# Gated values in PSUM banks, a bank seeded by a bank copy, and a new order of products and down products

## The chip, the cores and the metric

The kernel runs on one core of a Trainium2 chip. The metric is the device time of one execution in microseconds. Before the change it was 1130.64 us, the median of three runs (1128.69 to 1130.8).

## What is computed

A masked attention is followed by two gated feed-forward layers over 2304 tokens of 512 features, with 1536 hidden units in 12 chunks of 128. The second layer has no norm. Cut to what matters here:

```python
def _moe2_ref(x, w_gate, w_val, w_out):
    g = x @ w_gate
    silu = g * (1.0 / (1.0 + np.exp(-g)))
    val = x @ w_val
    return silu * val @ w_out
```

All is float32. The kernel makes each factor of a product the sum of a high and a low part (`xh` and `xl`, `hh` and `hl`, two planes of a weight tile) and multiplies three of the four pairs.

## The kernel before

The first part of the program runs the attention together with chunks 0 to 5 of the first layer. The change doesn't touch it. The second part goes through a list `work` of 15 blocks. A block is 768 tokens with a group of chunks: two passes of three chunks for the rest of the first layer (`m` is 1), then three passes of four chunks for the second (`m` is 2), each pass over three blocks of tokens. Block n uses one set of four PSUM banks for its chunks (`gv`) and the other (`ya`) for the down products of its first half; they change places at the next block.

A `Chunk` computes gate and value for the two halves of 384 tokens with seven products instead of eight, by sums of blocks of x and of the weights. `step(i)` issues product i, six matmuls, and what hangs on it. A chunk has two banks, x and y. Products 1, 6, 7 and 4 go to x one upon the other, and ScalarE copies x out in between (`keep`, L985): t1 after 1, t2 after 6, t3 after 7. Product 2 starts y anew; VectorE adds y to t1 (`add`, L990), and ScalarE makes silu of it (L994), which is the gate of the first half. Product 5 starts y anew again; y is added to t3, the value of the second half. Product 3 goes on top of 5; y is added to t2, the value of the first half. After product 4 ScalarE makes silu of x into t4, the gate of the second half. `join` multiplies gate and value on VectorE (L998), ScalarE rounds the result to `hh` (L1002), and VectorE makes the difference `hl` (L1003).

`Half.down` multiplies `hh` and `hl` of a half with a slice j of the down weights and sums over the chunks in bank y[j]; the last chunk's call adds what the pass before left (`evict`, L1080), in a tile `ob` that `fetch` (L1053) has filled from DRAM, and stores it (L1097). The x of the next block is loaded by `stage_x` (L939, one buffer), summed on POOL (L946, L947) and split product by product (`split_q`): ScalarE writes `xh` (L961), POOL makes sums (L955, L957) and `xl` (L962). Between these the weights of the next pass are decoded in steps that `point()` starts: DMA, ScalarE (L184, L185), VectorE (L190, L191), POOL (L235), ScalarE (L195), VectorE (L199).

The order of the code sets most of the order on each engine; a scheduler moves instructions within it by priorities (`ahead`, `behind`). Every engine, and the DMA queue of SP, serves its instructions in order. For one chunk and the next the order before is: product 1 of the next, 7 of this, 2 of the next, 6 of the next, 4 of this, 5 of the next, 3 of this, with down products between. At the last chunk 7, 4 and 3 follow with the down products of an earlier chunk between 7 and 4.

Of the kernel before, what the change touches and what calls it, by code (L numbers as in the profile page):

```python
# [25 lines left out]
def attn_ffn_ffn(ctx: ExitStack, tc: tile.TileContext, q, k, v, w1g, w1v, w1o, rms_g, w2g, w2v, w2o, out):  # L26
    nc = tc.nc
# [901 lines left out]
    x7, xs, tp, obp = (pools[key][0] for key in ("x7", "xs", "t", "ob"))  # L929
# [38 lines left out]
    class Chunk:  # L968
# [19 lines left out]
        @ahead  # L988
        def add(self, t):
            last["dve"] = ins_of(nc.vector.tensor_tensor(out=t, in0=t, in1=self.y[:, :HN], op=ALU.add))  # L990
# [5 lines left out]
        @ahead  # L996
        def join(self, s, v, half):
            nc.vector.tensor_tensor(out=s, in0=s, in1=v, op=ALU.mult)  # L998
            n = (3, 4)[half]
            hh = tp.tile([128, HN], F32R, tag=f"hh{half}", name="hh", bufs=n)  # L1000
            hl = tp.tile([128, HN], F32R, tag=f"hl{half}", name="hl", bufs=n)
            last["act"] = ins_of(nc.scalar.copy(out=hh, in_=s))  # L1002
            last["dve"] = ins_of(nc.vector.tensor_tensor(out=hl, in0=s, in1=hh.bitcast(F32), op=ALU.subtract))  # L1003
            return hh, hl

        def step(self, i):
            if i == 1:
# [3 lines left out]
                self.ga = self.keep("t1", 3)  # L1011
            elif i == 2:
                self.y = bank(self.tags[1])
                self.mult(self.y, 2, True)
                self.add(self.ga)
                self.silu(self.ga, self.ga)
            elif i == 6:
                self.mult(self.x, 6, False)
                self.va = self.keep("t2", 2)
            elif i == 5:  # L1020
                self.y = bank(self.tags[1])
                self.mult(self.y, 5, True)
            elif i == 7:
                self.mult(self.x, 7, False)
                self.vb = self.keep("t3", 2)
                self.add(self.vb)
            elif i == 4:
                self.mult(self.x, 4, False)
                gb = tmp("t4", 1)
                self.silu(gb, self.x[:, :HN])  # L1030
                self.hb = self.join(gb, self.vb, 1)
            elif i == 3:
                self.mult(self.y, 3, False)
                self.add(self.va)
                self.ha = self.join(self.ga, self.va, 0)
            point()

    class Half:

        def __init__(self, m, t0, tags, cs, before, after):  # L1040
# [4 lines left out]

        @ahead
        def fetch(self, j):
            if self.before is None:
                return
            ob = self.ob[j] = obp.tile([128, 512], F32, tag="ob", name="ob")  # L1050
# [24 lines left out]
        def evict(self, j):  # L1075
# [5 lines left out]
            else:  # L1081
                ob = obp.tile([128, 512], F32, tag="ob", name="ob")
# [21 lines left out]
    for n, (m, cs, t0) in enumerate(work):  # L1104
# [7 lines left out]
        halves = [Half(m, t0, ya, cs, before, after), Half(m, t0 + HN, gv[other:] + gv[:other], cs, before, after)]  # L1112
# [3 lines left out]
        def lower(c, js):  # L1116
            for j in js:
                halves[0].down(c.c, j, c.ha)
            point()
# [5 lines left out]
        def head_step(c, z):  # L1125
# [4 lines left out]
        def tail_step(c, z):  # L1130
            c.step(z)
            if c is chunks[-1]:
                split_next(z)

        def lower_at(i, js):
            if i >= 0:
                lower(chunks[i], js)

        def spread(js):
            for j in js:  # L1140
                for c in chunks[:-1]:
                    halves[1].down(c.c, j, c.hb)
                point()

        for z in (1, 2, 6):
            chunks[0].step(z)
            if left:
                left.pop(0)()
        for i, c in enumerate(chunks[:-1]):
            c1 = chunks[i + 1]  # L1150
            head_step(c1, 1)
            if i == 0:
                c.step(5)
                if nxt:
                    cell = stage_x(nxt[0], nxt[2])
                    sum_x(cell)
            tail_step(c, 7)
            head_step(c1, 2)
            lower_at(i - 2, J[:2])
            head_step(c1, 6)  # L1160
            tail_step(c, 4)
            head_step(c1, 5)
            tail_step(c, 3)
            lower_at(i - 2, J[2:])
            if t0 + 2 * HN == NT:
                used((m, c.c, False))
        for j in J:
            halves[0].fetch(j)
        tail_step(chunks[-1], 7)
        lower_at(k - 3, J)  # L1170
        tail_step(chunks[-1], 4)
        tail_step(chunks[-1], 3)
        if t0 + 2 * HN == NT:
            used((m, cs[-1], False))
        spread(J[:2])
        lower_at(k - 2, J)
        spread(J[2:])
        if t0 + 2 * HN == NT:
            for c in cs[:-1]:
                used((m, c, True))  # L1180
        lower_at(k - 1, J)
        for j in J:
            halves[1].fetch(j)

        def tailpiece(hf, c, js, done):
# [8 lines left out]
        def finished(m=m, c=cs[-1], t0=t0):  # L1194
            if t0 + 2 * HN == NT:
                used((m, c, True))

        js = [list(J[:2])] + [[j] for j in J[2:]]
        left = [tailpiece(halves[1], chunks[-1], g, finished if g is js[-1] else None) for g in js]
        left.pop(0)()  # L1200
        if nxt is None:
            while left:
                left.pop(0)()
# [31 lines left out]
```

## Time and profile before

| | |
|---|---|
| median of three runs | 1130.64 us |
| the profiled execution's own time | 1125.63 us |
| its span | 1123.9 us |
| TensorE matmul, weight load | 1018.3 us (91%), 919.3 us (82%) |
| VectorE | 721.1 us (64%) |
| ScalarE | 583.3 us (52%) |
| POOL | 484.1 us (43%) |
| DMA | 133.85 MB, 119 GB/s on the mean |

PE is TensorE's matmul, PEld its weight load, DVE VectorE, ACT ScalarE, POOL GpSimd, SP the queue that issues the DMAs. L66 is the line that issues every matmul. Matmuls overlap, so the duration of one is longer than the time from one start to the next, and a busy TensorE is not one at its peak. An instruction's row says how long its engine was idle ahead of it and what ended that.

### The profile page before, as it was taken

To read this page: it belongs to the slowest core of one execution; us is meant where nothing else is said; L and a number is where in the kernel's file an instruction comes from. 1 tells how busy PE (TensorE), PEld (TensorE's weight loads), DVE (VectorE), ACT (ScalarE), POOL (GpSimd) and SP (SyncE) were. 2 spreads that over 40 slices of the span, in tenths; PEclk is the share of its full clock that TensorE was granted. 3 is DMA by queue.
4 is the path that set the end of the run, shared out by engine and by line. 5 is a ranking of instruction groups with operands and counts; after the bars stand their busy time and mean duration, and the time that the engine had idled before them with its cause. 6 is when DMAs were issued, how large, how long until landed. Compare 5 with 4: busy or idle time off the path is not lost.

```text
span 1123.9 us, 16427 instructions
## 1 busy us (share of the span) xinstructions
PE 1018.3 (91%) x5804; PEld 919.3 (82%) x5804; DVE 721.1 (64%) x1361; ACT 583.3 (52%) x1435; POOL 484.1 (43%) x407
## 2 busy tenths in 40 slices
PE   5769999999999997998799799999889998979997
PEld 4569998777898787988699688879777987979896
DVE  3687464454436787669965887446978458894543
ACT  5877656366235573454634655436563427462431
POOL 3213112021001345667756848273856355583700
PEclk8758999999999998998899999999899999899999
DMA  7683152231233453353463271321253341615032
GB/s 198 174 225 104 61 159 65 80 98 38 61 118 114 149 160 96 111 184 123 163 199 121 74 234 39 131 93 58 85 178 114 130 146 61 207 55 169 2 113 75
DMA packets 130090, 133.85 MB, mean 119 GB/s; under 512 B 41428, under 2 KB 113820, under 8 KB 130008
## 3 DMA queue, kind: packets, MB, share of 16 engines
q1 hardware_dynamic: 129816, 132.53, 37.5%
q8 instruction: 45, 0.74, 0.3%
q0 software_dynamic: 192, 0.28, 0.1%
q14 instruction: 37, 0.30, 0.1%
HBM read 99.75 MB, written 33.03 MB: 118 GB/s over the span
## 4 chain that ended last, share of the span: by engine, by line
PE 45%; DVE 20%; DMA 16%; ACT 7%; POOL 6%; issue 3%; SPq 2%; DVEq 0%; ACTq 0%; POOLq 0%
PE b_y L66 16%; PE b_a L66 10%; PE b_g L66 9%; PE b_v L66 9%; DMA raw<-in_moe_w_out_dram 4%; POOL xl L962 4%; DMA part<-ob 4%; DVE t L998 3%; DVE hl L1003 3%; DVE dh L191 3%; DVE raw L190 3%; DVE w L199 3%; DMA ob<-part 2%; DVE t L990 2%; PE b_a L69 2%
## 5 line engine op out<-in xcount | busy, mean ns | idle before, releaser
L962 POOL TENSOR_TENSOR xl<-xst,xh 128x384 fp32r<-128x384 f32 x168 | 211.8, 1285 | 118.7 <-PE b_y L66 54.5
L66 PE MATMUL b_y<-xh,w 128*128 128x384 f32 x700 | 193.0, 346 | 31.2 <-DVE t L990 21.0
L66 PEld LDWEIGHTS b_y<-xh,w 128*128 128x128 f32 x700 | 130.7, 193 | 39.2 <-DVE t L990 25.3
L66 PE MATMUL b_g<-xh,w 128*128 128x384 f32 (+2 forms) x496 | 150.4, 351 | 7.1 <-ACT t L985 6.0
L66 PE MATMUL b_v<-xh,w 128*128 128x384 f32 (+2 forms) x432 | 132.5, 356 | 13.8 <-DVE t L990 13.8
L66 PE MATMUL b_a<-xh,w 128*128 128x384 f32 (+2 forms) x460 | 131.9, 341 | 13.6 <-DVE t L990 7.6
L998 DVE TENSOR_TENSOR t<-t,t 128x384 f32<-128x384 f32 x108 | 102.9, 955 | 49.2 <-ACT t L994 47.9
L1003 DVE TENSOR_TENSOR hl<-t,hh 128x384 fp32r<-128x384 f32 x108 | 107.3, 1004 | 25.8 <-ACT hh L1002 25.2
L66 PE MATMUL b_y<-hh,w 128*128 128x256 f32 (+2 forms) x432 | 120.1, 349 | 1.8 <-ACT hh L744 1.8
L66 PE MATMUL b_y<-xl,w 128*128 128x384 f32 x350 | 119.5, 341 | 0.0
L66 PEld LDWEIGHTS b_g<-xh,w 128*128 128x128 f32 x496 | 91.9, 193 | 16.7 <-ACT t L985 8.0
L66 PEld LDWEIGHTS b_a<-xh,w 128*128 128x128 f32 x460 | 84.5, 190 | 19.8 <-DVE t L990 9.5
L66 PEld LDWEIGHTS b_v<-xh,w 128*128 128x128 f32 x432 | 81.0, 196 | 22.7 <-DVE t L990 16.7
L487 POOL TENSOR_TENSOR e<-e,rc 128x384 f32<-128x384 f32 (+3 forms) x40 | 37.8, 949 | 134.6 <-DVE rc L481 62.4
L961 ACT CAST xh<-xst 128x384 fp32r<-128x384 f32 x180 | 83.4, 514 | 13.5 <-POOL xst L957 5.0
L190 DVE SCALAR_TENSOR_TENSOR raw<-raw 128x512 uint32<-128x512 uint32 x72 | 72.3, 1013 | 27.9 <-ACT raw L185 27.8
L66 PEld LDWEIGHTS b_y<-hh,w 128*128 128x128 f32 x432 | 79.6, 194 | 8.3 <-ACT hh L744 2.2
L1002 ACT CAST hh<-t 128x384 fp32r<-128x384 f32 x108 | 55.4, 514 | 59.1 <-DVE t L998 58.8
L66 PE MATMUL b_g<-xl,w 128*128 128x384 f32 (+2 forms) x248 | 84.4, 340 | 0.0
L235 POOL TENSOR_TENSOR raw<-dh 128x256 f32<-128x256 f32 x36 | 36.1, 1024 | 108.1 <-DVE dh L191 108.1
L66 PE MATMUL b_a<-xl,w 128*128 128x384 f32 (+2 forms) x230 | 77.9, 339 | 0.0
L66 PE MATMUL b_y<-hl,w 128*128 128x256 f32 (+2 forms) x216 | 74.1, 343 | 0.9 <-DVE hl L745 0.9
(186 smaller groups left out, 2263.7 us busy)
## 6 DMA issues: line engine op xcount, KB each, us to landing
xst<-y_d SPq DMA_DIRECT2D x18, 768.0 KB
raw<-in_moe_w_gate_dram SPq DMA_DIRECT2D x24, 512.0 KB
raw<-in_moe_w_val_dram SPq DMA_DIRECT2D x24, 512.0 KB
raw<-in_moe_w_out_dram SPq DMA_DIRECT2D x24, 512.0 KB
part<-ob SPq DMA_DIRECT2D x48, 256.0 KB
ob<-part SPq DMA_DIRECT2D x36, 256.0 KB
ob<-part SPq DMA_DIRECT2D x32, 192.0 KB
part<-ob SPq DMA_DIRECT2D x24, 192.0 KB
```

Of the source, the lines that this page charges most:

```text
L66: traced(nc.tensor.matmul(out_, a, b_, start=start, stop=stop, **how))
L69: traced(nc.tensor.transpose(out_, a, one))
L190: nc.vector.scalar_tensor_tensor(out=r, in0=cell["hw"], scalar=0x80000000, in1=r, op0=ALU.bitwise_and, op1=ALU.bitwise_or)
L191: nc.vector.scalar_tensor_tensor(out=h, in0=h, scalar=3, in1=r, op0=ALU.logical_shift_left, op1=ALU.bitwise_or)
L199: nc.vector.tensor_tensor(out=t[:, 1], in0=src, in1=t[:, 0].bitcast(F32), op=ALU.subtract)
L235: nc.gpsimd.tensor_tensor(out=t[:, z], in0=a, in1=b, op=ALU.subtract)
L487: eng.tensor_tensor(out=e[:qn, :nt, :kn], in0=e[:qn, :nt, :kn], in1=rc[:qn, :nt].unsqueeze(2).to_broadcast([qn, nt, kn]), op=ALU.mult)
L961: nc.scalar.copy(out=xh[:, kk], in_=src[:, kk])
L962: eng.tensor_tensor(out=xl[:, kk], in0=src[:, kk], in1=xh[:, kk].bitcast(F32), op=ALU.subtract)
L998: nc.vector.tensor_tensor(out=s, in0=s, in1=v, op=ALU.mult)
L1002: last["act"] = ins_of(nc.scalar.copy(out=hh, in_=s))
L1003: last["dve"] = ins_of(nc.vector.tensor_tensor(out=hl, in0=s, in1=hh.bitcast(F32), op=ALU.subtract))
```

## The change

Product 1 is copied by ScalarE from bank x into bank y (`seed`, L992 of the new kernel), and product 2 accumulates on it there, so that the add to t1 goes; silu reads bank y and writes t1. Product 4's silu and product 3's add write back to their banks instead of t4 and t2, and `join` takes the bank as its first factor: the product is written to the bank, `hh` is rounded from the bank, and the difference reads bank and `hh`. The banks are so held until `hl` is made. t1 has two buffers for three, t4 is gone. The other half's `ob` tiles 0 to 2 come from a pool of their own, `ob2`. The loop over the chunks is written anew: 4 and 3 of a chunk follow product 1 of the next, then 2, 6, 5 and 7 of the next, with groups of down products of both halves between; the second half's down products are put off into the block that follows.

```diff
+    open_pool("ob2", "ob2", 512, bufs=3)
...
+        def seed(self):
+            self.y = bank(self.tags[1])
+            last["act"] = ins_of(nc.scalar.copy(out=self.y[:, :HN], in_=self.x[:, :HN]))
...
+        def add(self, out_, t):
+            last["dve"] = ins_of(nc.vector.tensor_tensor(out=out_, in0=t, in1=self.y[:, :HN], op=ALU.add))
...
         def join(self, s, v, half):
+
+            s = s[:, :HN]
             nc.vector.tensor_tensor(out=s, in0=s, in1=v, op=ALU.mult)
...
-                self.ga = self.keep("t1", 3)
+                self.seed()
             elif i == 2:
-                self.y = bank(self.tags[1])
-                self.mult(self.y, 2, True)
-                self.add(self.ga)
-                self.silu(self.ga, self.ga)
+                self.mult(self.y, 2, False)
+                self.ga = tmp("t1", 2)
+                self.silu(self.ga, self.y[:, :HN])
...
-                gb = tmp("t4", 1)
-                self.silu(gb, self.x[:, :HN])
-                self.hb = self.join(gb, self.vb, 1)
+                self.silu(self.x[:, :HN], self.x[:, :HN])
+                self.hb = self.join(self.x, self.vb, 1)
             elif i == 3:
                 self.mult(self.y, 3, False)
-                self.add(self.va)
-                self.ha = self.join(self.ga, self.va, 0)
+                self.add(self.y[:, :HN], self.va)
+                self.ha = self.join(self.y, self.ga, 0)
...
+        def room(self, j):
+            return (self.pool if j < 3 else obp).tile([128, 512], F32, tag="ob", name="ob")
...
+        for z in (1, 0, 0, 2, 6, 0, 5, 7, 0):
+            step(chunks[0], z) if z else blank()
+        for i, c in enumerate(chunks[:-1]):
+            c1 = chunks[i + 1]
+            step(c1, 1)
+            step(c, 4)
+            step(c, 3)
...
+            step(c1, 2)
+            if i == 0 and nxt:
+                cell = stage_x(nxt[0], nxt[2])
+                sum_x(cell)
+            step(c1, 6)
+            blank()
+            lower(i - 1, 1)
+            step(c1, 5)
+            step(c1, 7)
+            if i == k - 2:
+                for j in J:
+                    halves[0].fetch(j)
             while left:
-                left.pop(0)()
+                blank()
+            lower(i, 0)
+        c = chunks[-1]
+        step(c, 4)
+        step(c, 3)
...
+        left = [piece(halves[1], c, g, other_done if g is G[-1] and c is chunks[-1] else None) for g in G for c in chunks]
+        lower(k - 2, 1)
+        blank()
+        blank()
+        for j in J:
+            halves[1].fetch(j)
+        lower(k - 1, 0)
+        lower(k - 1, 1)
+        blank()
```

Here `step` also splits x of the next block at the last chunk, `lower(i, g)` issues the first half's down products of chunk i for group g of the slices (two groups), and `blank` issues one put-off piece of the second half's.

Three places of the order show it. The first is TensorE in the first block, from the end of product 7 of its last chunk (w_8_3) to the start of product 4 on the same bank `b_g`; `b_y` are banks of down products. Before:

```order
L66 MATMUL b_g<-xh,w_8_3_4395 128x384
L66 MATMUL b_y_4795<-hh,w_6_2_4226 128x384 x2
L66 MATMUL b_y_4795<-hl,w_6_2_4226 128x384
L66 MATMUL b_y_4799<-hh,w_6_2_4226 128x384 x2
L66 MATMUL b_y_4799<-hl,w_6_2_4226 128x384
L66 MATMUL b_y_4803<-hh,w_6_2_4226 128x384 x2
L66 MATMUL b_y_4803<-hl,w_6_2_4226 128x384
L66 MATMUL b_y_4807<-hh,w_6_2_4226 128x384 x2
L66 MATMUL b_y_4807<-hl,w_6_2_4226 128x384
L66 MATMUL b_g<-xh,w_8_3_4395 128x384
```

Now, at the same place:

```order
L66 MATMUL b_g<-xh,w_8_3_4395 128x384
L66 MATMUL b_y_4685<-hh,w_7_2_4297 128x384 x2
L66 MATMUL b_y_4685<-hl,w_7_2_4297 128x384
L66 MATMUL b_y_4689<-hh,w_7_2_4297 128x384 x2
L66 MATMUL b_y_4689<-hl,w_7_2_4297 128x384
L66 MATMUL b_g<-xh,w_8_3_4395 128x384
```

Between 7 and 4 stood twelve down matmuls of the chunk two before; now six of the chunk before stand there.

The second place is VectorE in the second block, its first chunk and the start of the second (`t_` are SBUF tiles, `b_y` banks). Before:

```order
L990 TENSOR_TENSOR t_5004<-t_5004,b_y_4984 128x384
L990 TENSOR_TENSOR t_4982<-t_4982,b_y_5007 128x384
L998 TENSOR_TENSOR t_5030<-t_5030,t_5004 128x384
L1003 TENSOR_TENSOR hl<-t_5030,hh 128x384
L990 TENSOR_TENSOR t_4973<-t_4973,b_y_4984 128x384
L998 TENSOR_TENSOR t_4944<-t_4944,t_4973 128x384
L1003 TENSOR_TENSOR hl<-t_4944,hh 128x384
```

Now, the first chunk alone:

```order
L996 TENSOR_TENSOR t_4984<-t_4984,b_y_4971 128x384
L1006 TENSOR_TENSOR b_y_4920<-b_y_4920,t_4984 128x384
L996 TENSOR_TENSOR b_y_4971<-t_4957,b_y_4971 128x384
L1006 TENSOR_TENSOR b_y_4971<-b_y_4971,t_4949 128x384
L1011 TENSOR_TENSOR hl<-b_y_4920,hh 128x384
L1011 TENSOR_TENSOR hl<-b_y_4971,hh 128x384
```

The add of product 2 (the second row before, of the chunk that follows) is gone, and products and differences have a bank among their operands.

The third place is SP at the end of the program, the fetches and stores of the last block (`part` 1536 is its first half, 1920 its second). Before:

```order
L1053 DMA ob<-part_1536_2_4_9802 128x512
L1053 DMA ob<-part_1920_0_4_9820 128x512
L1097 DMA out_dram<-ob 128x512 x3
L1053 DMA ob<-part_1920_1_4_9826 128x512
L1097 DMA out_dram<-ob 128x512
L1053 DMA ob<-part_1920_2_4_9856 128x512
L1097 DMA out_dram<-ob 128x512 x2
```

Now:

```order
L1063 DMA ob<-part_1536_2_4_9711 128x512
L1107 DMA out_dram<-ob 128x512 x2
L1063 DMA ob<-part_1920_0_4_9753 128x512
L1063 DMA ob<-part_1920_1_4_9759 128x512
L1107 DMA out_dram<-ob 128x512
L1063 DMA ob<-part_1920_2_4_9879 128x512
L1107 DMA out_dram<-ob 128x512 x6
```

All fetches now stand ahead of the six stores of the last block.

## Rows read from the trace of the kernel before

**Rows 1.** The page: TensorE's granted clock in 40 slices, tenths of full.

```profile
PEclk8758999999999998998899999999899999899999
```

**Rows 2.** The chain that ended last: start us, us, what; 384 columns, then 512.

```profile
486.80 2.08 PE b_a L66 x12
...
1056.97 5.44 PE b_y L66 x24
```

**Rows 3.** Busy time by stretch: the second block, one decoding block, the nine's sum.

```profile
core 0: us, PE busy (x) PEld busy (x) DVE busy (x) ACT busy (x) POOL busy (x), PEclk, DMA share, GB/s
443.40:479.00 35.60, 34.88 (x200) 34.25 (x199) 22.10 (x29) 15.02 (x33) 18.81 (x14) 1.00 0.42 133
...
970.50:1023.50 53.00, 47.16 (x241) 42.46 (x240) 41.83 (x52) 27.25 (x58) 30.12 (x22) 1.00 0.43 144
sum 457.50, PE 397.48 PEld 367.20 DVE 357.62 ACT 248.19 POOL 293.72; mean PE 44.16 PEld 40.80 DVE 39.73 ACT 27.58 POOL 32.64
```

**Rows 4.** Waits of TensorE from 397 us on: total us, times, longest.

```profile
PE b_y L66 <- DVE t L990: 21.0, 11, 5.7
...
PE b_a L66 <- DVE t L990: 7.6, 6, 3.0
PE b_g L66 <- ACT t L985: 6.0, 5, 2.5
...
PE b_a L66 <- ACT t L985: 3.6, 3, 1.6
```

**Rows 5.** Timeline around the longest wait, and busy time by stretch, columns as above.

```profile
506.61 2.61 DVE L998 TENSOR_TENSOR t<-t,t 128x384 f32<-128x384 f32 x2
...
510.56 0.54 DVE L990 TENSOR_TENSOR t<-t,b_v 128x384 f32<-128x384 f32 x1
...
511.15 0.69 PE L66 MATMUL b_v<-xh,w 128*128 128x384 f32 x1 [5.71 <-DVE t L990]
...
504.80:511.20 6.40, 0.69 (x5) 0.37 (x3) 6.40 (x7) 2.62 (x6) 6.40 (x5) 0.67 0.21 73
511.20:517.10 5.90, 5.90 (x19) 5.90 (x20) 5.75 (x6) 2.78 (x7) 5.56 (x5) 0.50 0.00 0
```

**Rows 6.** Single lines of VectorE: ns min/median/max, first and last start us, forms.

```profile
L998 DVE TENSOR_TENSOR t<-t,t x108: 545/732/2210, 411.6 to 1104.6; 128x384 f32<-128x384 f32 x108
...
L1003 DVE TENSOR_TENSOR hl<-t,hh 128x384 fp32r<-128x384 f32 x108 | 107.3, 1004 | 25.8 <-ACT hh L1002 25.2
L998 DVE TENSOR_TENSOR t<-t,t 128x384 f32<-128x384 f32 x108 | 102.9, 955 | 49.2 <-ACT t L994 47.9
...
L990 DVE TENSOR_TENSOR t<-t,b_y x75: 540/547/556, 446.3 to 1058.6; 128x384 f32<-128x384 f32 x75
```

**Rows 7.** The nine decoding blocks' sums, of L998 and then of L1003 alone.

```profile
sum 457.50, DVE 64.72; mean DVE 7.19
...
sum 457.50, DVE 64.77; mean DVE 7.20
```

**Rows 8.** Groups of ScalarE: the bank copy, busy us and mean ns.

```profile
L985 ACT COPY t<-b_y 128x384 f32<-128x384 f32 x75 | 35.8, 479 | 65.1 <-PE b_y L66 64.8
```

**Rows 9.** Timeline of VectorE at the end of the program.

```profile
1118.98 0.69 DVE L1080 TENSOR_TENSOR ob<-ob,b_v 128x512 f32<-128x512 f32 x1 [3.36 <-DMA ob<-part]
```

**Rows 10.** POOL from 397 us on: waits for x, then groups with mean ns.

```profile
POOL s L946 <- DMA xst<-y_d: 74.7, 9, 11.4
...
POOL s L946 <- DMA xst<-x_d: 28.4, 4, 12.8
...
L962 POOL TENSOR_TENSOR xl<-xst,xh 128x384 fp32r<-128x384 f32 x168 | 211.8, 1285 | 118.7 <-PE b_y L66 54.5 <-ACT xh L961 37.9 <-PE b_g L66 25.7
...
L957 POOL TENSOR_TENSOR xst<-xst 128x768 f32<-128x768 f32 x14 | 29.8, 2128 | 0.2
L235 POOL TENSOR_TENSOR raw<-dh 128x256 f32<-128x256 f32 x30 | 29.0, 985 | 38.8 <-DVE dh L191 38.8
```

**Rows 11.** The wait of ScalarE's weight casts for POOL, in the same list of waits.

```profile
ACT w L195 <- POOL raw L235: 22.1, 14, 6.7
```

More of the change, by code (lines that the diff above doesn't have):

```diff
@@ L928, in attn_ffn_ffn @@
     open_pool("xs", "xs", 0, bufs=1, reuse_waits="tile")
-    x7, xs, tp, obp = (pools[key][0] for key in ("x7", "xs", "t", "ob"))
+    open_pool("ob2", "ob2", 512, bufs=3)
+    x7, xs, tp, obp, obq = (pools[key][0] for key in ("x7", "xs", "t", "ob", "ob2"))
     SETS = (("g", "v", "a0", "a1"), ("y0", "y1", "y2", "y3"))
@@ L988, in add @@
         @ahead
-        def add(self, t):
-            last["dve"] = ins_of(nc.vector.tensor_tensor(out=t, in0=t, in1=self.y[:, :HN], op=ALU.add))
+        def seed(self):
+            self.y = bank(self.tags[1])
+            last["act"] = ins_of(nc.scalar.copy(out=self.y[:, :HN], in_=self.x[:, :HN]))
+        @ahead
+        def add(self, out_, t):
+            last["dve"] = ins_of(nc.vector.tensor_tensor(out=out_, in0=t, in1=self.y[:, :HN], op=ALU.add))
         @ahead
@@ L1111, in attn_ffn_ffn @@
         other = 2 * (k % 2)
-        halves = [Half(m, t0, ya, cs, before, after), Half(m, t0 + HN, gv[other:] + gv[:other], cs, before, after)]
+        halves = [Half(m, t0, ya, cs, before, after, obp), Half(m, t0 + HN, gv[other:] + gv[:other], cs, before, after, obq)]
         nxt = work[n + 1] if n + 1 < len(work) else None
         J = range(halves[0].n)
[L1116 to L1119, printed above, removed]
+        G = [J[:2], J[2:]]
         def split_next(i):
@@ L1123, in split_next, with step @@
                 split_q(cell, i)
-        def head_step(c, z):
+        def step(c, z):
             c.step(z)
@@ L1128, in head_step, with lower, piece @@
                 split_next(z)
[L1130 to L1135, printed above, removed]
-            if i >= 0:
[L1137 to L1142, printed above, removed]
-                point()
-        for z in (1, 2, 6):
-            chunks[0].step(z)
-            if left:
-                left.pop(0)()
[L1149 to L1185, printed above, removed]
+        def lower(i, g):
+            if i >= 0:
+                for j in G[g]:
+                    halves[0].down(chunks[i].c, j, chunks[i].ha)
+                point()
+        def piece(hf, c, js, done):
             def f():
@@ L1192, in tailpiece, with other_done, blank @@
             return f
-        def finished(m=m, c=cs[-1], t0=t0):
+        def other_done(m=m, cs=cs, t0=t0):
             if t0 + 2 * HN == NT:
[L1196 to L1201, printed above, removed]
-            while left:
-                left.pop(0)()
+                for c in cs:
+                    used((m, c, True))
+        def blank():
+            if left:
+                left.pop(0)()
+        for z in (1, 0, 0, 2, 6, 0, 5, 7, 0):
[5 more added lines that the diff above has]
+            step(c, 3)
+            if t0 + 2 * HN == NT:
+                used((m, c.c, False))
+            step(c1, 2)
[10 more added lines that the diff above has]
+                    halves[0].fetch(j)
+            while left:
+                blank()
[3 more added lines that the diff above has]
+        step(c, 3)
+        if t0 + 2 * HN == NT:
+            used((m, c.c, False))
+        left = [piece(halves[1], c, g, other_done if g is G[-1] and c is chunks[-1] else None) for g in G for c in chunks]
[7 more added lines that the diff above has]
+        blank()
+        while nxt is None and left:
+            blank()
     close_pools(*reversed(list(opened)))
```

9 lines of the change are left out of this document (5 added, 4 removed).

## The prediction

> **What bounds the kernel now.** I read the page first. The span is 1123.9 us, and in slices of it the granted clock falls below full [rows 1]. The change touches only the second part of the program, from 397.8 us on: 15 blocks of 768 tokens, six of three chunks and then nine of four. A chunk is 42 matmuls of 384 columns for its seven products, and its down products are 24 of 384 columns (first FFN) or 18 of 512 (second). At full clock twelve of 384 take 2.08 us, 0.1735 us each, and 24 of 512 take 5.44 us, 0.227 us each [rows 2]. So a three-chunk block needs 3 x 66 x 0.1735 = 34.35 us of TensorE and a four-chunk block 4 x (42 x 0.1735 + 18 x 0.227) = 45.5 us. All 15 need 615.6 us. The trace has 718.5 us between 397.8 us and the last matmul, which ends near 1116.3 us, so 103 us are lost.
>
> Then I cut the stretch by blocks. The second block takes 35.6 us, 1.3 over its need, and VectorE is busy for 22.1 us of it. Nine blocks, those in which weights of the next pass are decoded, take 457.5 us together, where they need 4 x 34.35 + 5 x 45.5 = 364.9: they lose 92.6 us, nearly all there is. VectorE is busy for 357.6 us in them, 78% [rows 3].
>
> Then the waits of TensorE: 42.4 us of 25 waits end with the add at L990, 14.9 us with the bank copies at L985, the rest is small [rows 4]. The add only carries the delay. Before the longest wait (5.71 us, to 511.15) VectorE is busy for all of 6.4 us, and so is POOL: decoding, two products of L998, decoding, and only then the add of 0.54 us. Behind the wait the matmuls run for 5.9 us at a granted clock of 0.50, the lower level of 1.2 GHz, another 3 us lost [rows 5]. So the loss is VectorE's load in the decoding blocks, put into a queue that serves in order.
>
> What that load is made of decides the change. The add takes 540 to 556 ns in the 75 runs on the y banks (and no other in the 87 on the rest); it reads one operand from PSUM. The product L998 and the difference L1003 read two from SBUF: they take 545 ns at best and over 2200 at worst, 955 and 1004 on average [rows 6]. In the busy stretch two products took 2.61 us and the add 0.54 [rows 5].
>
> **The change, part by part.** *Products and differences in PSUM.* Each chunk's two products now read a bank and one SBUF tile and write the bank, and the two differences read the bank and one SBUF tile. No row has VectorE writing PSUM; the nearest are the adds that read it, 547 ns, and the bounds are that and the means of now, 955 and 1004. I take 547, since it is the same operation with its operand in the same memory. In the nine blocks L998 is busy for 64.72 us and L1003 for 64.77 [rows 7]; 128 of them at 0.547 are 70.0. This saves 59.5 us of VectorE.
>
> The Trainium skill (Trace Analysis, section Optimizing Scalar/DVE Operations) gives VectorE about 60 ns of access overhead per instruction on SBUF and about 125 on PSUM, which speaks against the change. Here the add with a PSUM operand has a median of 547 ns, and the product without one takes 545 at best, so the trace does not agree. By the page the 128 would cost 8 us more, an estimate, and the time would come out 8 us higher.
>
> *The seed.* Product 1 is copied from bank to bank by ScalarE, where it was copied to SBUF (L985, 479 ns [rows 8]), and product 2 accumulates on it. ScalarE's count stays. No row has ScalarE writing PSUM; I take the same 0.48 us, between nothing and twice that. VectorE loses one add a chunk: 32 x 0.547 = 17.5 us in the nine blocks.
>
> *Sum for VectorE.* 59.5 + 17.5 = 77.0 us of its 357.6 in these blocks. A block can't fall below its need: a four-chunk block's share is 77 x 4/32 = 9.6, and the one from 970.5 us loses only 7.5 [rows 3]. I cut 3 in all for such blocks and keep 74. VectorE's pauses are left as they are. The clean blocks get nothing: there TensorE is the bound.
>
> *The order of the products.* What was one product's cover mostly grows: between 7 and 3 of a chunk that isn't the last stand a down group, the next chunk's 1, and 4 (18 matmuls, 3.1 us). At the last chunk it shrinks: only 6 down matmuls and product 4, 2.1 us, where 12 and product 4 gave 3.1. The work behind it, a copy of 0.48 and an add of 0.55, still fits, with some 0.9 us to spare for whatever stands ahead of the add. Product 2 now waits for the seed, behind 4 and 3 of the chunk before (2.08 us). In the first block nothing stands between 1 and 2 of its first chunk: 0.9 us once. The copies of now gate 108 products and cost 14.9 us [rows 4], 0.14 us each; 54 seeds at about half of that are 4 us, as the new order leaves more cover than the old.
>
> *Down products and ob2.* The same matmuls, spread over more places. The second half gets three buffers of its own, so its partial sums can be fetched before the first half has been stored. At the end of the program VectorE waits 3.36 us for one of the last two fetches, until the last matmul is over [rows 9]; in the new order of SP they stand ahead of the last six stores. That is 4 us off the tail. The stage of the next x is written later in the block, but its DMAs stand on SP where they stood, among the stores and fetches of the block's start; I cost it at nothing, and the cover is what the first rival is about.
>
> *Sum.* 1125.6 us (span 1123.9 and 1.7 around it) - 74 - 4 + 0.9 + 4 = 1052.5. The median of the timed runs, 1130.6, lies 5 above this execution, so I put the new median at 1057.
>
> **The rivals.** *POOL becomes the bound in the three-chunk blocks.* POOL waits 103.1 us in 13 waits for x (7.9 each), makes four sums of 768 columns of up to 2.13 and 14 differences of 1.29 [rows 10]: 34.5 us a block, next to TensorE's 34.35, with one buffer for x. Eight decoding sums of 0.985 make it 42.4. The four decoding three-chunk blocks would be 38 long by my sum (their part of the 457.5 is 184.2, less 12/32 of 77 and some more: 150 to 155) and would then stay at 42.4, 169.6: some 17 us back, 1074. For it: POOL has no slack on paper. Against: the sums can lie in its wait for x, and 35.6 us has been run in a block without decoding.
>
> *All of it is gained.* The new covers hold everything, and with no waits the granted clock stays full: 103 + 4 off, 1125.6 - 107 + 5 = 1024.
>
> *The freed time is not what is missing.* The add of the last chunk still stands behind decoding steps, with 1 us less cover. If one wait of 5.7 us stays in each of the nine blocks, with the 3 us of low clock behind it [rows 5], that is 8.7 x 9 = 78 us: no change, 1131. Against: the queue ahead of that add has four long SBUF operations fewer per chunk.
>
> *Slower: the seeds.* ScalarE's queue also holds casts of weights that wait for POOL, 22.1 us in 14 waits, the longest 6.7 [rows 11]. A seed behind such a cast stops product 2, which before had a bank of its own. It decides from 1.4 us per seed (54 x 1.4 = 76). Were all 14 holds 6.7 us and at a seed, each would cost 4.6 beyond its cover and 3 at the low clock: 106 us, 32 more than the 74 gained, 1161. Against: their mean is 1.6 us, under the cover.
>
> **How the numbers follow.** Forecast 0.58, POOL 0.17, all gained 0.10, freed time not missing 0.08, seeds 0.07. The forecast alone spans 1040 to 1074: from the cap and the seeds at nothing, to the page's price and a few us of waits left. With POOL (1074, more if its waits for x don't shorten) and part of the case of all gained, 1034 to 1090 holds 8 in 10. Runs of this kernel can tell about 0.2% from no change: faster 0.89, same 0.04, slower 0.07.
>
> **What would show it.** Products and differences near 0.55 us with little spread, and VectorE's busy time down by about 120 us over the part, show the first step; near 0.95 refutes it. The block from 479 us should take about 37 us; at 42 with TensorE or ScalarE waiting for POOL, the first rival holds. TensorE's waits for the add should fall from 42 us below 15. A total of waits for the seed copy above 20 us means the cover is too short. The last store should be issued about 1 us after the last matmul. I am wrong if writes to PSUM take VectorE much longer, or if TensorE waits for xh or xl of the next block.

## The result, and the profile after

The changed kernel takes 1065.29 us in the median (four runs, 1064.08 to 1067.4), where the kernel before takes 1130.72: a ratio of 0.9426, with a 95% interval of 0.9406 to 0.9446. The forecast was 1057, the range 1034 to 1090. The profiled execution itself took 1065.94 us.

The page of the changed kernel, busy time of each engine and the clock row that answers to [rows 1]:

```profile
PE 999.3 (94%) x5804; PEld 906.3 (85%) x5804; DVE 592.2 (56%) x1307; ACT 575.4 (54%) x1435; POOL 436.9 (41%) x407
...
PEclk9858999999999989998999899999999999999999
```

VectorE was busy for 721.1 us before and is for 592.2 now, with 54 instructions fewer: the adds of the 54 chunks. POOL fell as well, from 484.1 to 436.9, though nothing of its work was changed.

Busy time by stretch, for the second and third block and for the nine decoding blocks together (answers to [rows 3]), and for the whole second part; x counts instructions:

```profile
core 0: us, PE busy (x) PEld busy (x) DVE busy (x) ACT busy (x) POOL busy (x), PEclk, DMA share, GB/s
...
433.60:467.90 34.30, 34.30 (x199) 34.30 (x198) 13.83 (x27) 15.43 (x35) 21.70 (x19) 1.00 0.43 138
467.90:512.50 44.60, 37.38 (x199) 35.54 (x199) 31.26 (x40) 23.89 (x51) 27.53 (x22) 0.92 0.40 125
...
sum 405.00, PE 379.24 PEld 353.13 DVE 271.55 ACT 241.05 POOL 249.31; mean PE 42.14 PEld 39.24 DVE 30.17 ACT 26.78 POOL 27.70
...
397.00:1064.00 667.00, 637.46 (x3353) 597.56 (x3352) 370.86 (x588) 344.72 (x747) 360.88 (x310) 0.98 0.40 131
```

The whole second part of the kernel before, for comparison:

```profile
397.00:1123.90 726.90, 652.78 (x3351) 607.44 (x3349) 498.56 (x643) 352.00 (x747) 407.70 (x310) 0.96 0.37 121
```

The second block now stands at its need of 34.35 us. The nine decoding blocks take 405.0 us where they took 457.5, so 52.5 us came from there. VectorE's busy time in them fell by 86.1 us, from 357.6 to 271.55. 40.1 us above the need of 364.9 are left in them; the third block alone holds 10. Of the 52.5 us, 34.3 are idle time of TensorE that went; the other 18.2 are busy time of the same matmuls (397.48 us before, 379.24 now). Before, the granted clock was below full in seven of the nine blocks, down to 0.89; now it is in five, down to 0.92. So with a wait that goes, slower matmuls behind it can go too ([rows 5] has some at 0.50).

What TensorE waits for from 397 us on (total us, times, longest; answers to [rows 4]):

```profile
PE b_a L66 <- DVE t L996: 7.4, 2, 5.6
PE b_y L66 <- DVE t L996: 7.1, 3, 4.0
...
PE b_v L66 <- ACT b_v L992: 0.9, 2, 0.6
PE b_y L66 <- ACT b_y L992: 0.5, 1, 0.5
```

In the kernel before, the third row of the waits for the add, beside the 21.0 and 7.6 us of [rows 4], is this:

```profile
PE b_v L66 <- DVE t L990: 13.8, 8, 5.7
```

Waits for the add fell from 42.4 us to 14.7 (7.4, 7.1 and one of 0.2); the seeds (L992) cost 1.4 us in all.

The operations that the change touches, by line and form (busy us and mean ns behind the bar; answers to [rows 6], [rows 8] and [rows 10]):

```profile
L963 POOL TENSOR_TENSOR xl<-xst,xh 128x384 fp32r<-128x384 f32 x168 | 179.2, 1098 | 67.1 <-ACT xh L962 65.3
...
L1006 DVE TENSOR_TENSOR b_y<-b_y,t 128x384 f32<-128x384 f32 x50 | 27.8, 562 | 33.2 <-ACT b_y L1000 32.6
...
L1011 DVE TENSOR_TENSOR hl<-b_y,hh 128x384 fp32r<-128x384 f32 x50 | 27.2, 551 | 9.3 <-ACT hh L1010 8.7
...
L992 ACT COPY b_y<-b_y 128x384 f32<-128x384 f32 x25 | 11.7, 467 | 36.8 <-PE b_y L66 36.7
```

Products and differences take 0.56 and 0.55 us, where they took 0.955 and 1.004. POOL's differences for `xl` take 1098 ns where they took 1285. That the long times came with POOL's work alongside can be read from the kernel before, in its last block, where POOL does nothing (the lines, then the busy time of that stretch):

```profile
L998 DVE TENSOR_TENSOR t<-t,t 128x384 f32<-128x384 f32 x8 | 4.5, 558 | 10.5 <-ACT t L994 10.3
L1003 DVE TENSOR_TENSOR hl<-t,hh 128x384 fp32r<-128x384 f32 x8 | 4.5, 558 | 4.0 <-ACT hh L1002 3.9
...
1069.70:1116.30 46.60, 46.56 (x244) 43.10 (x242) 19.22 (x35) 13.37 (x28) 0.00 (x0) 1.00 0.23 75
```

With POOL at 0.00 the same operations with two SBUF operands take 558 ns, no more than with a bank among them. Sorted one by one over the whole part, the trace of the kernel before says the same: the 39 products and 32 differences during which POOL ran nothing took 545 to 560 ns each, and the 59 and 69 that had POOL beside them for nine tenths of their time or more took 1257 and 1221 ns on the mean. In the changed kernel, sorted in the same way, the two means differ by 2 ns at most. The Trainium skill (SBUF — State Buffer, section Who interferes with whom) says that a VectorE instruction with two SBUF inputs contends with a GpSimd instruction that reads SBUF; the rows agree, 558 ns without POOL and 955 to 1004 on the mean of the whole part.

At the end of the program, VectorE of the changed kernel (answer to [rows 9]):

```profile
1060.26 0.69 DVE L1090 TENSOR_TENSOR ob<-ob,b_a 128x512 f32<-128x512 f32 x1 [2.03 <-PE b_a L66]
```

The last eviction now waits for TensorE and not for a fetch. Behind the end of the last matmul, at 1060.22 us, stand 3.7 us, where 7.6 stood.

### The profile page after: what moved, and what is told of

It reads as the page before. It is cut to its first block, busy times and chain, and to the rows that moved or that the text cites. A ratio compares the mean times of both kernels' runs of the same rounds, so it can differ in the third digit from the quotient of the medians.

```text
span 1064.0 us, 16342 instructions
## 1 busy us (share of the span) xinstructions
PE 999.3 (94%) x5804; PEld 906.3 (85%) x5804; DVE 592.2 (56%) x1307; ACT 575.4 (54%) x1435; POOL 436.9 (41%) x407
## 4 chain that ended last, share of the span: by engine, by line
PE 66%; DVE 12%; DMA 9%; ACT 6%; POOL 4%; issue 2%; SPq 1%; ACTq 0%; DVEq 0%; POOLq 0%
PE b_y L66 25%; PE b_a L66 16%; PE b_g L66 12%; PE b_v L66 11%; DVE raw L190 3%; DVE dh L191 3%; DMA raw<-in_moe_w_out_dram 3%; DMA raw<-in_moe_w_val_dram 3%; PE b_a L69 2%; DVE w L199 2%; POOL raw L235 2%; ACT dh L184 1%; POOL xl L963 1%; ACT raw L185 1%; DMA raw<-in_moe_w_gate_dram 1%
## 5 line engine op out<-in xcount | busy, mean ns | idle before, releaser
L963 POOL TENSOR_TENSOR xl<-xst,xh 128x384 fp32r<-128x384 f32 x168 | 179.2, 1098 | 67.1 <-ACT xh L962 65.3
L66 PE MATMUL b_y<-xh,w 128*128 128x384 f32 x700 | 192.3, 340 | 10.6 <-DVE t L996 7.1
L66 PE MATMUL b_a<-xh,w 128*128 128x384 f32 (+2 forms) x460 | 127.1, 339 | 9.0 <-DVE t L996 7.4
L66 PE MATMUL b_v<-xh,w 128*128 128x384 f32 (+2 forms) x432 | 130.1, 351 | 2.4 <-ACT t L1000 1.3
L235 POOL TENSOR_TENSOR raw<-dh 128x256 f32<-128x256 f32 x36 | 32.9, 934 | 137.6 <-DVE dh L191 137.6
L66 PEld LDWEIGHTS b_y<-hh,w 128*128 128x128 f32 x432 | 78.1, 191 | 11.2 <-ACT hh L744 3.8
L190 DVE SCALAR_TENSOR_TENSOR raw<-raw 128x512 uint32<-128x512 uint32 x72 | 65.9, 924 | 23.9 <-ACT raw L185 23.3
L947 POOL TENSOR_TENSOR s<-xst 128x768 f32<-128x768 f32 x14 | 26.1, 1866 | 123.8 <-DMA xst<-y_d 75.6
L66 PE MATMUL b_v<-xl,w 128*128 128x384 f32 (+2 forms) x216 | 73.4, 340 | 0.0
L470 ACT ACTIVATE e<-e,nb 128x96 f32<-128x96 f32 (+2 forms) x152 | 56.5, 375 | 23.4 <-DVE nb L461 23.3
```

The source lines that it names most:

```text
L66: traced(nc.tensor.matmul(out_, a, b_, start=start, stop=stop, **how))
L190: nc.vector.scalar_tensor_tensor(out=r, in0=cell["hw"], scalar=0x80000000, in1=r, op0=ALU.bitwise_and, op1=ALU.bitwise_or)
L235: nc.gpsimd.tensor_tensor(out=t[:, z], in0=a, in1=b, op=ALU.subtract)
L470: r = nc.scalar.activation(out=e[:qn, i, :kn], in_=e[:qn, i, :kn], func=AF.Exp, bias=nb[:qn, i:i + 1], scale=-1.0, accum_out=sums[:qn, i:i ...
L947: g(out=s1, in0=cell["a21"], in1=cell["a22"], op=ALU.add)
L963: eng.tensor_tensor(out=xl[:, kk], in0=src[:, kk], in1=xh[:, kk].bitcast(F32), op=ALU.subtract)
```

## The experiments

The runs stand in three groups, in the order of this table by four; the kernels of a group ran on one chip beside the kernel before, which measured 1128.7, 1128.5 and 1128.0 us there. Ratios are to it.

| run | order of products | product, difference | seed | ob2 | median us | ratio, 95% interval |
|---|---|---|---|---|---|---|
| e5_order_only | new | SBUF | no | no | 1128.07 | 0.9985 (0.9958 to 1.0011) |
| e3_psum_old_order | old | bank | yes | no | 1129.33 | 1.0009 (0.9986 to 1.0032) |
| e4_one_ob | new | bank | yes | no | 1059.7 | 0.9400 (0.9369 to 0.9430) |
| e1_sbuf_joins | new | SBUF | yes | no | 1114.21 | 0.9879 (0.9847 to 0.9912) |
| r_changed_again | new | bank | yes | yes | 1066.95 | 0.9447 (0.9410 to 0.9485) |
| r_one_ob_again | new | bank | yes | no | 1060.58 | 0.9387 (0.9337 to 0.9436) |
| e2_no_seed | new | bank | no | no | 1058.81 | 0.9378 (0.9340 to 0.9416) |
| e6_decode_held | new | bank | yes | no | 1071.2 | 0.9485 (0.9442 to 0.9529) |
| e3a_old_order_banks_free | old | bank, SBUF | yes | no | 1121.39 | 0.9946 (0.9926 to 0.9965) |
| e3b_old_order_no_seed | old | bank | no | no | 1118.09 | 0.9923 (0.9893 to 0.9954) |
| e1b_sbuf_differences | new | bank, SBUF | yes | no | 1079.84 | 0.9577 (0.9542 to 0.9611) |
| e7_x_first | new | bank | yes | no | 1059.5 | 0.9398 (0.9369 to 0.9426) |

The theory under test is the forecast's: VectorE's load in the decoding blocks sets the time, and the operands' place lowers it. Its rival is that the new order does it.

### The two halves apart

**The new order alone.** The chunk of the kernel before (adds, `t4`, products and differences in SBUF) in the new loop, without `ob2`. Against the changed kernel, cut:

```diff
-                self.seed()
+                self.ga = self.keep("t1", 3)
...
-                self.silu(self.x[:, :HN], self.x[:, :HN])
-                self.hb = self.join(self.x, self.vb, 1)
+                gb = tmp("t4", 1)
+                self.silu(gb, self.x[:, :HN])
+                self.hb = self.join(gb, self.vb, 1)
```

> The new order of products and down products alone: no seed, products and differences in SBUF as before, one ob pool. If VectorE's load in the decoding blocks is the cause (the theory of the forecast), that load is the old one (near 358 us in the nine blocks) and the time stays within 1105 to 1131. If the order is what removed the waits, the time is within 10 us of the run e4_one_ob, near 1075, although VectorE is as busy as before.

It took 1128.07 us, the time of the kernel before. VectorE's load is nearly the old one (489 us from 397 us on, 498.56 before). But TensorE's waits have changed:

```profile
PE b_y L66 <- DVE hl L1003: 16.7, 11, 3.0
PE b_y L66 <- DVE t L990: 16.7, 10, 2.6
PE b_g L66 <- DVE hl L1003: 15.1, 10, 3.0
```

Waits for the add fell to 29.0 us (with 7.8 and 4.5 on two more banks); but the new order issues the down products one chunk earlier, and they wait 31.8 us for `hl`: all 21 matmuls of these two rows read `hh` or `hl`. The order gives cover in one place and takes it in another.

**The other half alone.** The seed, and products and differences in the banks, in the old loop, without `ob2`. Against the changed kernel, cut:

```diff
-            step(c, 4)
-            step(c, 3)
+            head_step(c1, 6)
+            tail_step(c, 4)
+            head_step(c1, 5)
+            tail_step(c, 3)
```

> The old order of products and down products, with the seed and with products and differences in PSUM, one ob pool. If VectorE's load is the cause, its busy time falls by about 77 to 86 us in the nine blocks and the time is 1069 to 1090, the upper part of it if the banks, which are now held until the difference is made, come free too late for the old order. If the order is what counts, the time is 1110 or more.

It took 1129.33 us, again no change. This is the run that breaks the simple theory. Its busy time from 397 us on, and TensorE's waits:

```profile
397.00:1129.00 732.00, 649.46 (x3345) 598.20 (x3343) 367.05 (x586) 343.37 (x745) 362.89 (x310) 0.98 0.37 120
...
PE b_g L66 <- DVE hl L1010: 14.2, 8, 4.8
PE b_y L66 <- DVE hl L1010: 12.6, 11, 4.6
PE b_y L66 <- ACT b_y L991: 11.7, 10, 3.0
PE b_v L66 <- ACT b_v L991: 8.6, 8, 1.5
```

VectorE is busy for 367.05 us, less than in the changed kernel (370.86) and 131 less than before (498.56 from 397 us on). None of it became time. With the third pair of banks (2.9 and 5.2 us) TensorE waits 29.7 us for the difference (L1010) and 25.5 us for the seed (L991). None of the 24 matmuls that wait for the difference is a down product: they read `xh` and write a bank that the difference still reads, as product 1 of the chunk after next does. The timeline around the longest but one of these waits, VectorE and then TensorE:

```profile
532.34 0.55 DVE L1005 TENSOR_TENSOR b_y<-b_y,t 128x384 f32<-128x384 f32 x1
532.81 1.36 DVE L199 TENSOR_TENSOR w<-dh,w 128x512 fp32r<-128x512 f32 x1
...
534.55 0.55 DVE L995 TENSOR_TENSOR b_y<-t,b_y 128x384 f32<-128x384 f32 x1
535.02 0.55 DVE L1010 TENSOR_TENSOR hl<-b_y,hh 128x384 fp32r<-128x384 f32 x1
...
535.62 0.69 PE L66 MATMUL b_y<-xh,w 128*128 128x384 f32 x1 [4.57 <-DVE hl L1010]
```

Product 4 lies in the bank, and silu, product, rounding and difference must all be over before the bank can take product 1 of the chunk after next. Here the product (532.34) was late behind decode steps (one at 529.62 took 2.33 us), and the difference later still. In the old order 4, 5 of the next chunk and 3 stand last, and that product 1 follows behind 3 with at most one group of down products between. In the new order 4 and 3 come right behind product 1 of the next chunk, and its 2, 6, 5 and 7 and down products still lie between them and the chunk after next. The seed has less cover too: in the old order only product 7 of the chunk before (six matmuls) stands between product 1 and product 2, in the new one products 4 and 3 (twelve).

**Both halves, without ob2.** Cut:

```diff
-    open_pool("ob2", "ob2", 512, bufs=3)
...
-        halves = [Half(..., obp), Half(..., obq)]
+        halves = [Half(..., obp), Half(..., obp)]
```

> The changed kernel with the pool ob2 taken back: the second half's ob tiles come from the shared pool again. If ob2 is worth the tail alone, VectorE waits for the last fetches again as before (about 3.4 us) and the time is 1067 to 1070. If the shared pool also holds up evictions within the blocks, and with them banks, the time is 1074 or more and TensorE waits for VectorE's evictions there.

1059.7 us. Each half alone is worth nothing, both together 69 us. In this trace TensorE waits 0.8 us for the difference and 1.2 us for the seed: differences of 0.55 us are ready for the early down products, and the new order leaves time until a held bank is wanted again. Neither of the two times expected came: it is below 1067, and the next group takes that up.

**SBUF operands in the new order.** The same kernel, with the two products and the two differences of a chunk in SBUF again (cut):

```diff
-                self.hb = self.join(self.x, self.vb, 1)
+                gb = tmp("t4", 1)
+                self.silu(gb, self.x[:, :HN])
+                self.hb = self.join(gb, self.vb, 1)
```

> The new order and the seed, products and differences back in SBUF, one ob pool; against e4_one_ob it differs only in where gate, value and product lie. If products and differences with two SBUF operands are lengthened by POOL, their mean is near 1 us again, and the time is about 36 us above e4_one_ob (59.5 us of VectorE at the rate at which saved VectorE time became time, 52.5 of 86), near 1105. If where the operands lie does not matter once the order is new, it is within 5 us of e4_one_ob.

1114.21 us, 54.5 more. The two groups of VectorE:

```profile
L1009 DVE TENSOR_TENSOR hl<-t,hh 128x384 fp32r<-128x384 f32 x108 | 123.3, 1161 | 8.0 <-ACT hh L1008 7.5
L1004 DVE TENSOR_TENSOR t<-t,t 128x384 f32<-128x384 f32 x108 | 99.5, 926 | 79.9 <-ACT t L999 78.6
```

They are at 1 us again. In the new order the operands' place is worth 54.5 us, more than the 36 expected. Against e5_order_only this kernel has the seed in addition: it is worth 14 us here, in a kernel whose VectorE is nearly as loaded as before (470 us from 397 us on).

### ob2, the seed, and the decode steps

**The changed kernel and the one without ob2, side by side.**

> The changed kernel itself, beside the next three on the same chip. It gives the yardstick: 1062 to 1068.

> The changed kernel without the pool ob2, again, now beside the changed kernel. In the traces its last matmul ends 5.6 us earlier and its tail behind it is as long (3.8 us), so ob2 gives nothing at the end. If ob2 costs time within the blocks (more fetches on SP ahead of the next x), this kernel is 4 to 7 us below the changed one. If the difference of the first comparison was the chip's, they are within 2 us.

1066.95 and 1060.58: without ob2 the kernel is 6.4 us faster on one chip, and no run of the one reaches into those of the other (1065.03 to 1068.25, 1056.64 to 1063.1). The first comparison had 5.6, not beside each other, or 3 by the ratios. The tail is as long either way, 3.7 us. SP at the start of the third block, first the changed kernel, then the one without ob2:

```profile
469.47 1.88 SPq L1107 DMA_DIRECT2D part<-ob  x4
...
472.89 5.41 SPq L1063 DMA_DIRECT2D ob<-part  x8
478.40 1.20 SPq L940 DMA_DIRECT2D xst<-x_d  x2
...
480.85 0.74 SPq L940 DMA_DIRECT2D xst<-x_d  x1
```

```profile
466.43 1.88 SPq L1106 DMA_DIRECT2D part<-ob  x4
...
470.29 0.53 SPq L939 DMA_DIRECT2D xst<-x_d  x1
...
472.70 1.50 SPq L939 DMA_DIRECT2D xst<-x_d  x2
```

With free tiles in ob2 nine fetches pass ahead of x where four did, and x's last DMA goes out 11.4 us behind the first store instead of 6.8. POOL's sums start 18.3 us behind that store (487.74) instead of 13.4 (479.87). In this pair of traces that block takes 5.8 us longer with ob2, but other blocks are shorter: all 15 together differ by 1.9 us, and the first product of the second part already starts 3.9 us later (401.4 against 397.5). In the first pair the loss lay elsewhere (3 us in the sixth block, 2.2 in the tenth). So some 6 us are shown, but neither their place nor that the fetches ahead of x cause them.

**No seed in the new order.**

```diff
-                self.seed()
+                self.ga = self.keep("t1", 2)
...
-                self.mult(self.y, 2, False)
-                self.ga = tmp("t1", 2)
-                self.silu(self.ga, self.y[:, :HN])
+                self.y = bank(self.tags[1])
+                self.mult(self.y, 2, True)
+                self.add(self.ga, self.ga)
+                self.silu(self.ga, self.ga)
```

> The new order with products and differences in PSUM and one ob pool, but product 1 copied to SBUF again and added to product 2 by VectorE (no seed). If VectorE's load is what counts, its 17.5 us in the nine blocks come back at the rate of 52.5 of 86: about 11 us above the kernel without ob2, near 1071. If the seeds cost TensorE as much as they save VectorE, it is within 3 us of that kernel, or below it.

1058.81 against 1060.58: no difference that the intervals can tell. So the seed that gave 14 us with SBUF operands gives nothing once products and differences read banks. VectorE is 22 us busier than the 360.90 of the kernel with the seed, and no time follows (this kernel from 397 us on):

```profile
397.00:1055.10 658.10, 632.72 (x3344) 590.61 (x3342) 382.85 (x640) 344.54 (x743) 359.05 (x310) 0.99 0.41 133
```

**Decode steps held back.** While `hold` is set, `point()` starts no step of the decoding:

```diff
             elif i == 5:
+                state["hold"] = True
...
                 self.add(self.vb, self.vb)
+                state["hold"] = False
```

> The kernel without ob2, and decode steps held back while products 5 and 7 are issued, so that none of them is queued on VectorE or ScalarE between those products and the add of 7. If what is still lost (TensorE's waits for that add, 11.4 us, with the low clock behind them) comes from the queue of decode steps ahead of that add, the waits fall below 5 us and the time is 8 to 15 us below the kernel without ob2, near 1047. If the held steps only come up elsewhere (ahead of the products, or late for the weights), it is within 4 us of that kernel or above.

1071.2, 10.6 us slower. What was to fall fell: waits for the add went from 10.2 us of idle time (without ob2) to 5.1. But the held steps came up elsewhere:

```profile
PE b_g L66 <- DVE hl L1010: 3.6, 2, 2.5
PE b_y L66 <- ACT t L999: 3.6, 2, 2.7
PE b_a L66 <- ACT t L999: 2.9, 1, 2.9
...
PE b_y L66 <- DVE t L995: 2.5, 1, 2.5
```

TensorE now waits for silu (L999) and for the difference. Moved in this way within the block, the queue of decode steps ahead of one add delays something else.

### Why the old order gains nothing, and what is left

**Banks free after the product.** The old loop as in e3_psum_old_order, with the product written to the SBUF factor:

```diff
-            nc.vector.tensor_tensor(out=s, in0=s, in1=v, op=ALU.mult)
+            nc.vector.tensor_tensor(out=v, in0=s, in1=v, op=ALU.mult)
+            s = v
```

> The old order with the seed as in e3_psum_old_order, but the product of gate (in the bank) and value is written to SBUF, so that the bank is free after the product and not after the difference; the differences read two SBUF operands again. If the old order gained nothing because product 1 of the chunk after next waits for banks held until the difference (33.6 us of TensorE's waits there), these waits fall below 10 us and the time is 1095 to 1120 although VectorE is busier (108 differences at about 1 us). If the banks are not the reason, the longer differences make it 1130 or more.

(The 33.6 and 29.4 us in the expectations are counted from one matmul's start to the next; as idle time they are the 29.7 and 25.5 of the rows above.) It took 1121.39, 8 us less than e3_psum_old_order (7 by the ratios, as the two groups ran on different chips), and 1.4 above the span expected. The waits for the difference are gone from the head of the list, though VectorE is 44 us busier (411 us from 397 us on):

```profile
PE b_y L66 <- ACT b_y L991: 13.3, 10, 3.6
PE b_v L66 <- ACT b_v L991: 11.5, 8, 2.6
PE b_y L66 <- DVE t L995: 8.6, 5, 3.3
...
PE b_y L66 <- DVE t L1005: 4.8, 4, 3.1
```

So the held bank was one of its waits. The seeds still cost 28.7 us (3.9 of it on a third bank); the add, 14.7 us, and the product (L1005, now the bank's last reader), 7.7 us, have taken over the rest.

**No seed in the old order.** The edit of e2_no_seed in the old loop.

> The old order with products and differences in PSUM, but without the seed: product 1 is copied to SBUF and VectorE adds product 2 to it, as in the kernel before. If the seeds are the other part of the loss there (29.4 us of TensorE's waits for them), those waits go, VectorE gets 17.5 us more in the nine blocks, and the time is 1105 to 1118. If product 2 then waits for the same bank instead, it stays within 1125 to 1132.

1118.09, at the edge of the first expectation: 11.2 us less than with the seed (10 by the ratios). The waits for the held bank stay:

```profile
PE b_g L66 <- DVE hl L1010: 17.6, 9, 6.7
PE b_y L66 <- DVE hl L1010: 13.9, 13, 3.6
PE b_y L66 <- DVE t L995: 11.1, 7, 4.1
```

In the old order the seed costs some 10 us and in the new one nothing. With 3.9 us on a third bank, 35.4 us of TensorE's waits still end with the difference here, more than with anything else. But undoing either part gave only 7 to 11 us of the 70 that lie between the two orders, as other waits took over, and no run undoes both. That the held bank and the seed together are why the old order gains nothing is read from these waits; no run shows it in full.

**Differences alone back in SBUF.** The edit of e3a_old_order_banks_free in the new loop.

> The changed kernel without ob2, but the product is written to SBUF, so that the difference alone reads two SBUF operands; the bank is free sooner. If VectorE's load is what counts, the 30 us of the nine blocks that the differences gained come back, and with them about half of what putting both in SBUF cost (54.5): near 1087. If holding banks costs something in the new order too, it is below 1075.

1079.84, 20 us above the kernel without ob2 (against about 27 expected): the differences' share of the 54.5. The time lies between the two expectations, so the run can't tell whether the bank's earlier release gives a few us back.

**x first.**

```diff
+        if nxt:
+            cell = stage_x(nxt[0], nxt[2])
         for z in (1, 0, 0, 2, 6, 0, 5, 7, 0):
```

> The changed kernel without ob2, with the DMAs of the next x written ahead of the block's first product, and POOL's two sums behind the first chunk. If the rest of the loss in the decoding blocks is POOL's work on x falling together with the decoding, x lands some 4 us earlier there and the time is 1050 to 1057. If the fetches that now stand behind x come late for the evictions, or POOL's work only meets other decode steps, it is 1059 or more.

1059.5, ratio 0.9398, where the kernel without ob2 had 0.9400 and 0.9387: no change. But x didn't come 4 us earlier. On SP, x of the third block stands behind four stores and four fetches as it did without the edit, and POOL's sums start 11.7 us behind the block's first product, where they start 13.8 and 11.6 us behind it in the two runs without ob2. So the run says only that x's place in the code brings nothing; whether an x that lands earlier would, it leaves open.

## Why the prediction was right, and where it was not

The time lay within the range, 8 us above the forecast, in the forecast's case. In part that is luck: between the two profiled executions the gain is 59.7 us where the sum had 73.1, and 5 us that were added at the end hide some of the gap. Its main step held: products and differences that read a bank take 0.55 to 0.56 us (0.547 had been taken), VectorE's busy time fell by 86 us in the nine blocks (77 forecast) and by 128 over the part (about 120), and TensorE's waits for the add fell to 14.7 (below 15). In the new order this step is worth 54.5 us by e1_sbuf_joins. The rule of the Trainium skill that was weighed there (Perfetto Trace Analysis, section Optimizing Scalar/DVE Operations: about 65 ns more of access overhead for PSUM) isn't borne out: 551 and 562 ns with a bank, 558 without one and without POOL.

**The order of the products** is the step that failed as reasoning. It was priced as cover that "mostly grows", at little more than nothing. In fact it is the condition for all the rest: without it the time is 1129.33. The description of the change says that the banks are held until `hl` is made, and the prediction didn't price it: nowhere did it ask how long after product 4 the same bank is wanted again. Had the order been left, the working would have come out much the same, for a kernel that takes 1129. The rival *the freed time is not what is missing*, at 0.08, names what happens there, though by another mechanism (the add, not the bank).

**The sum for VectorE** turned 77 us of busy time, cut to 74, into 74 us of time. It was 52.5 for 86, about six tenths. The term supposed that every microsecond of VectorE in those blocks delays TensorE. Of the 25 us of waits that TensorE has left in the part, 14.7 end with an add, and the longest of them stands behind a burst of decode steps. The cap was too small as well: at 9.6 us for each four-chunk block, three blocks lose less than that before the change, by 3.9, 2.1 and 1.1 us, which is 7 and not 3. The third block, which was to take 37 us, takes 44.6. VectorE in the stretch before its longest wait (5.6 us, to 492.3), and the busy time of that stretch:

```profile
483.86 2.94 DVE L190 SCALAR_TENSOR_TENSOR raw<-raw 128x512 uint32<-128x512 uint32 x2 [1.77 <-ACT raw L185]
486.73 2.29 DVE L191 SCALAR_TENSOR_TENSOR dh<-dh,raw 128x512 uint32<-128x512 uint32 x1
488.94 1.48 DVE L190 SCALAR_TENSOR_TENSOR raw<-raw 128x512 uint32<-128x512 uint32 x1
...
491.74 0.54 DVE L996 TENSOR_TENSOR t<-t,b_a 128x384 f32<-128x384 f32 x1
...
484.10:492.30 8.20, 2.69 (x16) 2.37 (x14) 8.20 (x7) 3.98 (x9) 8.04 (x5) 0.78 0.30 94
```

It is the picture of [rows 5] without the products: five decode steps with two SBUF operands, and the add behind them. The first took 0.69 us, the other four, beside a busy POOL, 1.48 to 2.33.

**The seed** was costed at 4 us of waits and paid 1.4; but the 17.5 us of VectorE that it saves are worth nothing beside bank operands, as e2_no_seed shows. The load only counts while it makes something late.

**ob2** was credited with 4 us at the end. The gain is there (the tail fell from 7.6 to 3.7 us) but comes from the order: without ob2 the tail is as short, and in the old order with the new chunk it is 7.5. ob2 itself costs some 6 us, where the sum had nothing; the cause stays open.

**The clean blocks** were to get nothing; the six gained 4.6 us together (the second went from 35.6 to 34.3). **The 5 us** between profile and median, taken over from the kernel before, were not there: the profiled execution lay 0.65 us above the median.

**The rivals.** POOL as the bound didn't come: two of the four decoding three-chunk blocks lie above its 42.4 us (44.6 and 43.6) and two far below (34.8 and 36.8), and in the former TensorE waits for the add. The slower case, seeds behind ScalarE's casts, shows in the old order (25.5 us of waits for seeds) and hardly in the new one. Two prices of the rivals are a little off in themselves: 1130.6 and 32 make 1163 for the seeds, not 1161, and 1057 and 78 make 1135 for *the freed time*, not 1131.

**What stays open.** 40 us are still lost in the decoding blocks. Decode steps held back in two products (e6_decode_held) don't win them, whether POOL's work on x beside the decoding is their cause wasn't settled (e7_x_first), and what would win them wasn't found. The new order moves products 4, 3 and 7, brings the first half's down products forward and puts the second half's off, all at once; which of these is needed was not taken apart. The fastest kernels seen are the changed one without ob2, with or without the seed: 1058.81 to 1060.58 us, some 6 us below the changed kernel.

## What to carry to other kernels

When a value stays in a bank instead of being copied out, the bank's new last reader is part of the change: follow it to the next matmul on that bank and price the distance, before counting the engine time that is saved. Two edits that give nothing alone can give everything together, so a change of several parts should be judged by undoing them one by one, and the part that brings nothing (here the seed, once the operands lie in banks) or costs (here ob2) taken out. Saved busy time is worth at most what the waits behind it are worth.

## What was not expected of the hardware

POOL gained too: its differences for `xl` went from 1285 to 1098 ns, 33 us less over the part. Some 20 of these go with the operands alone: 1203 ns in e1_sbuf_joins and 1089 in the kernel without ob2, which differ in nothing but where gate, value and product lie. So the contention lengthens both sides. Writing a bank costs VectorE little: the product that reads and writes one takes 562 ns, the difference that only reads one 551. ScalarE's copy from bank to bank takes 467 ns, less than the 479 of the copy to SBUF [rows 8].
